# Attention with gradients: the usual path last in the branch, three loads per head in single gated bursts, two transposes of the tail ahead

## The chip, the cores and the metric

The kernel runs on one core of a Trainium2 chip. The metric is device time in microseconds (us), the median of the runs given with each number. Two kernels are compared only by runs of the same job, on the same chip, and kernels of different jobs by their ratios to the kernel before. A ratio is the mean time of one kernel's runs over the mean of the other's runs of the same rounds, so it is not quite the ratio of the medians that are quoted; its 95% interval follows it in brackets.

Engines: PE is the TensorE (matmul), PEld its weight loads, DVE the VectorE, ACT the ScalarE, POOL the GpSimd, SP the SyncE, which here issues all DMA transposes. L683 is line 683 of the kernel.

## The reference

One step of a network and all its gradients:

```python
# S = 2048 rows, D = 576, H = 32 heads of Dh = 128, F = 4608, bfloat16
def A(x, k_cache, v_cache, wq, wo):
    q = (x @ wq) split into heads
    p = softmax(q @ k^T * Dh**-0.5)
    o = p @ v
    return (o joined) @ wo
def forward(...):
    xn = layernorm(x)
    s = A(xn, ...)
    g = silu((sigmoid(xn @ w_gate) * (xn @ w_up)) @ w_down)
    return x + s * g
def reference(..., grad_out):          # forward, then jax.vjp of it:
    return out, dx, dK, dV, dwq, dwo, dw_gate, dw_up, dw_down
```

(The layout is shortened; what the argument needs is that each of 32 heads has a score part, which makes o, and a gradient part, which makes dq, dK and dV.)

## The kernel before

A head is worked in 32 **rows** (row tiles of 128 queries): 16 of scores, 16 of gradients. PE is the bound (busy 99% of the span); a head that nothing disturbs takes 94.63 us, 2.957 us a row. A *slab* is one row's 128 x 2048 of P (later dS). It is transposed by a DMA on the SP queue (PT, later dST), and six rows later (the skew) PE reads the transpose as weights in L683. The loads of the next head, the stores of this one and the transposes are fitted in between. Cuts are marked with `# ...`.

```python
def load_wo(hs):
    nf = (DT - 1) * P if KPAD else D               # 512 of the 576 columns
    rows = slice(hs.h * P, (hs.h + 1) * P)
    if nf:
        nc.gpsimd.dma_start(wo_h[:, :nf], A_wo[rows, :nf])        # L171: 128x512
    if KPAD:
        nc.gpsimd.dma_start(wo_h[:, nf + LO:], A_wo[rows, nf:])   # L173: 128x64
def turn_wot(hs):
    nc.sync.dma_start_transpose(hs.woT[:], wo_h[:])               # L208
# ...
def turn_nat(dst, src):                                           # KT<-Kn, VT<-Vn
    nc.sync.dma_start_transpose(dst..., src...)                   # L615
def transpose_slab(hs, qt, name):                                 # PT, dST
    nc.sync.dma_start_transpose(T[:], hs.slabs[qt][:])            # L630
# ...
# class Partial, end of dV (turned is KT) and of dK (turned is VT):
    nc.gpsimd.dma_start(self.out_T, self.turned)                  # L756: 512 KB to kvT_d
# ... plan(h): what is put into which slot; pl is row 16 of head h-1
put(pl, 0, lambda: heads.__setitem__(h, start_head(h)))
for c in range(4):
    put(pl + q(c), 0, lambda c=c: load_k(hd(), c, 4))             # Kn, 4 x 128 KB
    put(pl + q(skew + 3 + c), 0, lambda c=c: load_v(hd(), c, 4))  # Vn, 4 x 128 KB
put(pl + q(4), 0, lambda: load_wo(hd()))
put(pl + q(5), 0, lambda: load_wq(hd()))
put(pl + q(NTH + 3), 0, lambda: turn_nat(hd().KT, hd().Kn))
put(pl + q(skew + 4), 0, lambda: turn_wot(hd()))
# ...
with tc.If(flag > 0) as branch:
    attention(True)          # the usual path
with branch.Else():
    attention(False)
```

(Kn and Vn are K and V as loaded, KT and VT their transposes.)

Of the kernel before, what the change touches and what calls it, by code (L numbers as in the profile page):

```python
# [66 lines left out]
def kernel(  # L67
# [6 lines left out]
    nc = tc.nc  # L74
# [6 lines left out]
    NT = S // P  # L81
# [85 lines left out]
    def load_wo(hs):  # L167
        nf = (DT - 1) * P if KPAD else D
        rows = slice(hs.h * P, (hs.h + 1) * P)
        if nf:  # L170
            nc.gpsimd.dma_start(wo_h[:, :nf], A_wo[rows, :nf])  # L171
        if KPAD:
            nc.gpsimd.dma_start(wo_h[:, nf + LO:], A_wo[rows, nf:])  # L173
# [5 lines left out]
    def load_k(hs, c=0, n=1):  # L179
        load_kv(hs, hs.Kn, A_k_cache, c, n)  # L180

    def load_v(hs, c=0, n=1):
        load_kv(hs, hs.Vn, A_v_cache, c, n)
# [50 lines left out]
    with tc.tile_pool(name="pa", bufs=1) as pa:  # L234
# [265 lines left out]
        wo_h = pdT.tile([P, DT * P], bf, name="wo_h")  # L500
# [92 lines left out]
    def attention(fast):  # L593
        with ExitStack() as es:
# [169 lines left out]
            def put(slot, cols, fn):  # L764
                units.setdefault(slot, []).append((cols, fn))
# [18 lines left out]
            def q(k):  # L784
                return min(k, NT - 1)

            def plan(h):
                b1, b2 = 2 * NT * h, 2 * NT * h + NT
                hd = lambda: heads[h]
                pl = b2 - 2 * NT if h else None  # L790
                if h:
                    put(pl, 0, lambda: heads.__setitem__(h, start_head(h)))
                    for c in range(4):
                        put(pl + q(c), 0, lambda c=c: load_k(hd(), c, 4))
                        put(pl + q(skew + 3 + c), 0, lambda c=c: load_v(hd(), c, 4))
                    put(pl + q(4), 0, lambda: load_wo(hd()))
                    put(pl + q(5), 0, lambda: load_wq(hd()))
                    put(pl + q(NTH + 3), 0, lambda: turn_nat(hd().KT, hd().Kn))
                    put(pl + q(skew + 4), 0, lambda: turn_wot(hd()))
                    for sc in range(NSC):  # L800
                        put(pl + q(skew + 4 + 2 * sc), DT * CH, lambda sc=sc: prep_qt(hd(), sc))
                for qt in range(NT):
                    put(b1 + qt + skew, NT * P // 2, lambda qt=qt: tail1(hd(), qt, 0))
                    put(b1 + qt + skew, NT * P // 2, lambda qt=qt: tail1(hd(), qt, 1))
                for sc in range(NSC):
                    put(b1 + q(sc), DT * CH, lambda sc=sc: prep_dot(hd(), sc))
                    put(b1 + q(sc + 1), nb * P, lambda sc=sc: prep_don(hd(), sc))
                for qt in range(NT):
                    put(b1 + max(qt + 1, q(2 + qt // nb)), 0, lambda qt=qt: scale_don(hd(), qt))
                put(b1 + q(NTH + 3), 0, lambda: turn_nat(hd().VT, hd().Vn))  # L810
                put(b1 + q(NTH + 2), NT * P, lambda: prep_qn(hd()))
                for qt in range(NT):
                    put(max(b1 + qt + 1, b1 + NT - 4 + qt // 2 if qt < NTH else b1 + NT + qt), 0, lambda qt=qt: scale_qn(hd(), qt))
                put(b2 + 1, 0, lambda: post1(hd()))
                parts = {}

                def first(key, rhs, lo, hi, eng, factor=1.0):
                    parts[key] = part_tile()
                    return Partial(hd(), lo, hi, rhs, parts[key], None, None, eng, factor)
                spread(b1 + NTH, lambda: first("v", hd().dOn, 0, NTH, "v"))  # L820
                spread(b2, lambda: Partial(hd(), NTH, NT, hd().dOn, parts["v"], hd().KT, kvT_d[h, 1], None))
                spread(b2 + NTH, lambda: first("k", hd().Qn, 0, NTH, "s", SCALE))
                spread(b2 + NT, lambda: Partial(hd(), NTH, NT, hd().Qn, parts["k"], VT[:], kvT_d[h, 0], None, SCALE))
                for qt in range(NT):
                    put(b2 + qt + skew, NT * P // 2, lambda qt=qt: tail2(hd(), qt, 0))
                    put(b2 + qt + skew, NT * P // 2, lambda qt=qt: tail2(hd(), qt, 1))
# [37 lines left out]
                slot += 1  # L864

    flag = nc.values_load(flag_i[0:1, 0:1], min_val=0, max_val=1, skip_runtime_bounds_check_because="a comparison gives 0 or 1")
    with tc.If(flag > 0) as branch:
        attention(True)
    with branch.Else():
        attention(False)  # L870
    pdT.release()

    def late(name, bufs=1, **kw):
# [8 lines left out]
    with late("pc") as pc, late("pcf") as pcf, \  # L882
# [165 lines left out]
        def turn_rows(dst, src, a, b, n):  # L1048
            nc.sync.dma_start_transpose(dst[:, a * n:b * n, :], src[:, a:b, :].rearrange("p t f -> p (t f)"))  # L1049
# [111 lines left out]
        with late("c2w") as wp, late("c2b") as blk, late("c2s", 2) as sb, late("c2ps", 4, space=PSUM) as ps:  # L1161
# [10 lines left out]
            dqbT2 = blk.tile([P, max(1, NTE) * HG, P], bf, name="dqbT2")  # L1172
            wqT2 = blk.tile([P, HG, D], bf, name="wqT2")

            def dx_more(st, both=False):
                acc = ps.tile([P, WD], f32, name="acc")
                terms = [(dqbT[:, st * HG + hl, :], wqT[:, hl, :]) for hl in range(HG)]
                if both:
                    terms += [(dqbT2[:, st * HG + hl, :], wqT2[:, hl, :]) for hl in range(HG)]
                dx_row(acc, st, terms)  # L1180
                return acc
# [22 lines left out]
                nc.gpsimd.dma_start(o1[st * P:(st + 1) * P, :], dx[:])  # L1204

            NQ = max(1, NT // 4)
            for hg in range(NHG):
                cols = slice(hg * HC, (hg + 1) * HC)
                onb, dqb = onqs[hg % 2]
                final = hg == NHG - 1  # L1210
                early = hg == NHG - 2
                ends = list(range(NTE)) if early else list(range(NTE, NT)) if final else []
                nc.sync.dma_start_transpose(wqT, A_wq[:, cols])  # L1213
                def turn_dq(a, b):
                    for a_ in range(a, b, NQ):
                        turn_rows(dqbT, dqb, a_, min(a_ + NQ, b), HG)
                turn_dq(NTE if final else 0, NTE if early else NT)
                if early:
                    nc.sync.dma_start_transpose(wqT2[:], A_wq[:, (hg + 1) * HC:(hg + 2) * HC])
                    turn_rows(dqbT2, onqs[(hg + 1) % 2][1], 0, NTE, HG)  # L1220
                dwq = wp.tile([P, DT, HC], bf, name="dwq")
                for st in ends[:2]:
                    load_got(st)
                nsteps, step_n = 2 * HG, 0
                wait_n = min(3 if early else 1, nsteps - 2)
                todo_rows = list(ends)
                held = []

                def ends_rows():
                    if todo_rows and step_n >= wait_n:  # L1230
                        for _ in range(-(-len(todo_rows) // max(1, nsteps - step_n - final))):
                            if todo_rows:
                                st = todo_rows.pop(0)
                                finish(st, dx_more(st, early))
                                if st + 2 <= ends[-1]:
                                    load_got(st + 2)
                for hl in range(HG):
                    h = hg * HG + hl
                    lcols = slice(hl * P, (hl + 1) * P)
                    accumulate(ps.tile([P, WD], f32, name="acc"), dqb, xn_all, lcols, dqTs[h % 2])  # L1240
                    nc.sync.dma_start_transpose(dwq[:, :, lcols], dqTs[h % 2][:])
                    if early and hl == min(1, HG - 1):
                        turn_dq(NTE, NT)
                    if final and hl == HG - 1:
                        store_T(out_4, cols, dwq)
                    step_n += 1
                    ends_rows()
                    dwo = sb.tile([P, D], bf, name="dwo")
                    accumulate(ps.tile([P, WD], f32, name="acc"), onb, ds_all, lcols, dwo)
                    nc.gpsimd.dma_start(out_5[h * P:(h + 1) * P, :], dwo[:])  # L1250
                    step_n += 1
                    if hl < HG - 1:
                        ends_rows()
                if not final:
                    if hg + 2 < NHG:
                        load_on(onb, hg + 2)
                        load_dq(dqb, hg + 2)
                    store_T(out_4, cols, dwq)
                    for st in range(len(ends), NT):
                        acc = dx_more(st)  # L1260
                        nc.vector.tensor_tensor(dxn[:, st, :], acc[:, :D], dxn[:, st, :], op=ALU.add)
                while todo_rows:
                    step_n = nsteps
                    ends_rows()
# [30 lines left out]
```

## Time and profile before

| | before |
|---|---|
| median of 4 runs beside the changed kernel's | 4947.94 us (4942.96 to 4948.41) |
| span of the profiled run | 4943.52 us |
| start to first score tile | 482.91 us |
| heads 0 to 31, to the end of the attention | 3053.05 us |
| of it heads 1 to 30, over 30 x 94.63 us | 8.48 us |
| end of the attention to the end of the kernel | 1407.56 us |

The page's first parts, the stretches, PE's waits and the places of the three targets are in the prediction below. In such tables of waits the three numbers are total us, times, and the longest; in a timeline line the first two are start and length, and the bracket is the idle time just before with what ended it. This is the timeline of the kernel before, head 1 (it starts at 573.48 us), the queues of GpSimd and SP:

```profile
643.13 0.55 POOL L756 DMA_DIRECT2D kvT_d<-KQ  x1 [4.58 <-DVE KQ L754]
648.72 0.77 POOL L677 DMA_DIRECT2D dq_d<-dq_n  x1 [5.04 <-ACT dq_n L724]
651.00 2.83 SPq L615 DMA_TRANSPOSE KQ<-Kn  x1
653.92 18.67 SPq L630 DMA_TRANSPOSE dST<-Pq  x8
```

The dV store is issued at row (643.13 - 573.48) / 2.957 = 23.6, as soon as DVE has made dV. It has landed when the K transpose comes up at 651.00 (row 26.2), between the slab transposes, and nobody waits.

### The profile page before, as it was taken

To read this page: it belongs to the slowest core of one execution; us is meant where nothing else is said; L and a number is where in the kernel's file an instruction comes from. 1 tells how busy PE (TensorE), PEld (TensorE's weight loads), DVE (VectorE), ACT (ScalarE), POOL (GpSimd) and SP (SyncE) were. 2 spreads that over 40 slices of the span, in tenths; PEclk is the share of its full clock that TensorE was granted. 3 is DMA by queue.
4 is the path that set the end of the run, shared out by engine and by line. 5 is a ranking of instruction groups with operands and counts; after the bars stand their busy time and mean duration, and the time that the engine had idled before them with its cause. 6 is when DMAs were issued, how large, how long until landed. Compare 5 with 4: busy or idle time off the path is not lost. (4 is left out here: it accounts for less than half of the span.)

```text
span 4943.5 us, 101621 instructions
## 1 busy us (share of the span) xinstructions
PE 4877.6 (99%) x41029; PEld 2892.8 (59%) x41029; DVE 2802.9 (57%) x6554; ACT 2473.9 (50%) x4228; POOL 843.4 (17%) x1329
## 2 busy tenths in 40 slices
PE   9999999999999999999999999999899999999998
PEld 4445666666666666666666666666455555555554
DVE  4544666666566666666656666666434555554225
ACT  4431766766676676676666667667312111111011
POOL 3322111111111111111111111111221111111111
PEclk9999999999999999999999999999999999999999
DMA  7887999999999999999999999999999999998665
GB/s 260 274 202 173 225 222 225 228 229 230 222 231 224 230 225 237 219 227 220 235 220 231 233 224 229 231 221 231 210 225 235 223 234 218 233 226 204 195 168 151
DMA packets 3048181, 1097.68 MB, mean 222 GB/s; under 512 B 2951890, under 2 KB 2956115, under 8 KB 3047699
## 3 DMA queue, kind: packets, MB, share of 16 engines
q1 hardware_dynamic: 2948930, 771.66, 83.4%
q0 software_dynamic: 98160, 318.85, 20.3%
q8 instruction: 322, 5.28, 0.4%
q14 instruction: 161, 1.31, 0.1%
q10 hardware_dynamic: 608, 0.59, 0.0%
HBM read 175.31 MB, written 177.93 MB: 71 GB/s over the span
## 5 line engine op out<-in xcount | busy, mean ns | idle before, releaser
L654 ACT ACTIVATE Pq<-sp 128x1024 bf16<-128x1024 f32 x1024 | 1048.0, 1024 | 268.7 <-PE sp L636 259.4
L709 DVE SCALAR_TENSOR_TENSOR Pq<-dp,negdelta,Pq 128x1024 bf16<-128x1024 f32 x512 | 655.2, 1280 | 44.5 <-PE dp L706 44.5
L712 ACT ACTIVATE t<-dp,negdelta 128x1024 bf16<-128x1024 f32 x512 | 567.6, 1115 | 214.3 <-PE dp L706 199.8
L636 PE MATMUL sp<-KQ 128*128 128x512 bf16 x2048 | 609.6, 379 | 2.2 <-ACT Pq L654 2.1
L706 PE MATMUL dp<-VT,dOT 128*128 128x512 bf16 x2048 | 609.2, 379 | 2.3
L683 PEld LDWEIGHTS <-dST 128*128 128x128 bf16 x8192 | 506.8, 98 | 155.5 <-DMA dST<-Pq 16.3
L683 PEld LDWEIGHTS <-PT 128*128 128x128 bf16 x8192 | 499.8, 98 | 133.6 <-DMA PT<-Pq 14.1
L683 PE MATMUL acc<-Kn,dST 128*128 128x128 bf16 x8192 | 556.3, 219 | 9.0 <-DMA dST<-Pq 8.8
L683 PE MATMUL acc<-Vn,PT 128*128 128x128 bf16 x8192 | 542.0, 219 | 8.6 <-DMA PT<-Pq 8.3
L713 DVE TENSOR_TENSOR Pq<-t,Pq 128x1024 bf16<-128x1024 bf16 x512 | 354.6, 693 | 319.3 <-ACT t L712 307.0
L744 PE MATMUL acc<-Pq,dOn 128*128 128x512 bf16 x2048 | 531.1, 379 | 0.0
L744 PE MATMUL acc<-Pq,Qn 128*128 128x512 bf16 x2048 | 526.7, 380 | 0.0
L724 ACT ACTIVATE dq_n<-acc,rsc 128x128 bf16<-128x128 f32 x512 | 187.7, 367 | 335.1 <-PE acc L683 313.6
L1154 DVE TENSOR_TENSOR dxn<-acc,dxn 128x576 f32<-128x576 f32 x272 | 206.1, 758 | 248.1 <-PE acc L1054 248.1
L744 PEld LDWEIGHTS <-Qn 128*128 128x128 bf16 x2048 | 200.4, 98 | 240.8 <-issue 1.5
L744 PEld LDWEIGHTS <-dOn 128*128 128x128 bf16 x2048 | 198.9, 98 | 233.8
L1116 ACT ACTIVATE ndh<-dh 128x512 bf16<-128x512 f32 x144 | 86.0, 597 | 452.5 <-DVE du_blk L1114 448.7
L641 DVE TENSOR_REDUCE rs_all<-rsp 128x1 f32<-128x2 f32 x512 | 78.4, 153 | 306.4 <-ACT Pq L654 294.8
L636 PEld LDWEIGHTS <-KQ 128*128 128x128 bf16 x2048 | 179.3, 98 | 124.4 <-issue 4.0
L706 PEld LDWEIGHTS <-dOT 128*128 128x128 bf16 x2048 | 178.7, 98 | 124.6 <-issue 12.4
L677 POOL DMA_DIRECT2D on_d<-o_n x128 | 97.4, 761 | 784.3 <-DVE junk L695 460.3
L677 POOL DMA_DIRECT2D dq_d<-dq_n x128 | 98.2, 768 | 721.4 <-ACT dq_n L724 681.7
(208 smaller groups left out, 6827.6 us busy)
## 6 DMA issues: line engine op xcount, KB each, us to landing
out_dram<-kvn POOLq DMA_DIRECT2D x64, 512.0 KB, 4.8
ah<-a_d POOLq DMA_DIRECT2D x18, 1024.0 KB, 9.3
ah<-h_d POOLq DMA_DIRECT2D x18, 1024.0 KB, 11.7
h_d<-h_row POOLq DMA_DIRECT2D x64, 256.0 KB, 3.5
a_d<-a_row POOLq DMA_DIRECT2D x64, 256.0 KB, 3.9
x_all<-in_A_k_cache_dram SPq DMA_DIRECT2D x64, 256.0 KB, 4.0
on_d<-o_n POOLq DMA_DIRECT2D x128, 128.0 KB, 4.6
kvT_d<-KQ POOLq DMA_DIRECT2D x32, 512.0 KB, 5.7
```

The source lines that it names most:

```text
L636: nc.tensor.matmul(sp[:, c * CH:(c + 1) * CH], lhsT=hs.QT[:, qt * P:(qt + 1) * P], rhs=hs.KT[:, hf * HW_ + c * CH: hf * HW_ + (c + 1) * CH ...
L654: nc.scalar.activation(Pq[:, hsl], sp[:], AF.Exp, scale=SCALE, accum_out=hs.rsp[:, hf:hf + 1])
L677: nc.gpsimd.dma_start(dst_d[q0 * P:(qt + 1) * P, hs.h * P:(hs.h + 1) * P].rearrange("(t p) d -> p t d", p=P), buf[:])
L683: nc.tensor.matmul(hs.acc[:, 0, :], lhsT=T[:, kt, :], rhs=rhs[:, kt, :], start=(kt == 0), stop=(kt == NT - 1))
L706: nc.tensor.matmul(dp[:, c * CH:(c + 1) * CH], lhsT=hs.dOT[:, qt * P:(qt + 1) * P], rhs=hs.VT[:, hf * HW_ + c * CH: hf * HW_ + (c + 1) * C ...
L709: nc.vector.scalar_tensor_tensor(Pq[:, hsl], dp[:], hs.negdelta[:, qt:qt + 1], Pq[:, hsl], op0=ALU.add, op1=ALU.mult)
L712: nc.scalar.activation(t[:], dp[:], AF.Identity, bias=hs.negdelta[:, qt:qt + 1], scale=1.0)
L713: nc.vector.tensor_tensor(Pq[:, hsl], t[:], Pq[:, hsl], op=ALU.mult)
L724: nc.scalar.activation(hs.dq_n[:, qt % G4, :], hs.acc[:, 0, :], AF.Copy, scale=hs.rsc[:, qt:qt + 1])
L744: nc.tensor.matmul(self.acc, lhsT=self.nat[:, qt, :], rhs=self.slabs[qt][:, cs], start=(qt == self.lo), stop=(qt == self.hi - 1))
L1116: nc.scalar.mul(ndh[:], dh[:], -1.0)
L1154: nc.vector.tensor_tensor(dxn[:, st, :], acc[:, :D], dxn[:, st, :], op=ALU.add)
```

## The change

Its intent has three parts. **Loads:** K, wo with wq, and V of the next head each load in one burst, held to a row by a *gate*: a one-element copy on GpSimd from a slab of that row into the destination, so that the load is not issued earlier (K comes at a median row of 18.3, the first piece of wo at 21.8, V at 28.4); they are to stand apart from the dK and dV stores. **Branch:** the usual attention path comes last, so that it falls through into what follows and the jump stands at its entry. **Tail:** the last group's wq transpose and first dq transposes are issued earlier.

```diff
-                    for c in range(4):
-                        put(pl + q(c), 0, lambda c=c: load_k(hd(), c, 4))
-                        put(pl + q(skew + 3 + c), 0, lambda c=c: load_v(hd(), c, 4))
-                    put(pl + q(4), 0, lambda: load_wo(hd()))
-                    put(pl + q(5), 0, lambda: load_wq(hd()))
+                    def gated(slot, dst, fn):
+                        def run():
+                            nc.gpsimd.tensor_copy(dst(), heads[h - 1].slabs[slot % NT][0:1, 0:1])
+                            fn(hd())
+                        put(slot, 0, run)
+                    gated(pl + q(1), lambda: hd().Kn[0:1, 0, 0:1], load_k)
+                    gated(pl + q(5), lambda: wo_h[0:1, 0:1], lambda hs: (load_wo(hs), load_wq(hs)))
+                    gated(pl + q(skew + 6), lambda: hd().Vn[0:1, 0, 0:1], load_v)
 ...
-    with tc.If(flag > 0) as branch:
+    with tc.If(flag < 1) as branch:
+        attention(False)
+    with branch.Else():
         attention(True)
-    with branch.Else():
-        attention(False)
 ...
+            def last_turns():
+                nc.sync.dma_start_transpose(wqT2[:], A_wq[:, (NHG - 1) * HC:])
+                turn_rows(dqbT2, onqs[(NHG - 1) % 2][1], 0, NTE, HG)
 ...
-                if early:
-                    nc.sync.dma_start_transpose(wqT2[:], A_wq[:, (hg + 1) * HC:(hg + 2) * HC])
-                    turn_rows(dqbT2, onqs[(hg + 1) % 2][1], 0, NTE, HG)
 ...
+                if hg == NHG - 3:
+                    last_turns()
```

(Cut: the last group reads `wqT2` in place of a transpose of its own, and a case for two groups.)

More of the change, by code (lines that the diff above doesn't have):

```diff
@@ L1173, with dx_more @@
             wqT2 = blk.tile([P, HG, D], bf, name="wqT2")
-            def dx_more(st, both=False):
+            def last_turns():
+                nc.sync.dma_start_transpose(wqT2[:], A_wq[:, (NHG - 1) * HC:])
+                turn_rows(dqbT2, onqs[(NHG - 1) % 2][1], 0, NTE, HG)
+            def dx_more(st, both=False, w=wqT):
                 acc = ps.tile([P, WD], f32, name="acc")
-                terms = [(dqbT[:, st * HG + hl, :], wqT[:, hl, :]) for hl in range(HG)]
+                terms = [(dqbT[:, st * HG + hl, :], w[:, hl, :]) for hl in range(HG)]
                 if both:
@@ L1206 @@
             NQ = max(1, NT // 4)
+            if NHG == 2:
+                last_turns()
             for hg in range(NHG):
@@ L1212 @@
                 ends = list(range(NTE)) if early else list(range(NTE, NT)) if final else []
-                nc.sync.dma_start_transpose(wqT, A_wq[:, cols])
+                if not (final and NTE):
+                    nc.sync.dma_start_transpose(wqT, A_wq[:, cols])
                 def turn_dq(a, b):
@@ L1233, in ends_rows @@
                                 st = todo_rows.pop(0)
-                                finish(st, dx_more(st, early))
+                                finish(st, dx_more(st, early, wqT2[:] if final and NTE else wqT))
                                 if st + 2 <= ends[-1]:
@@ L1261 @@
                         nc.vector.tensor_tensor(dxn[:, st, :], acc[:, :D], dxn[:, st, :], op=ALU.add)
+                if hg == NHG - 3:
+                    last_turns()
                 while todo_rows:
```

## The prediction

> **What bounds the kernel now.** I read the page first, then the waits of the TensorE (PE) alone, then the stretches around its idle time, then the DMA issues around those.
>
> The page's first and second parts:
>
> ```profile
> span 4943.5 us, 101621 instructions
> PE 4877.6 (99%) x41029; PEld 2892.8 (59%) x41029; DVE 2802.9 (57%) x6554; ACT 2473.9 (50%) x4228; POOL 843.4 (17%) x1329
> PE   9999999999999999999999999999899999999998
> ```
>
> PE is idle for 4943.5 - 4877.6 = 65.9 us in all. The change keeps every matmul, so only this idle time, and the half-speed clock that follows it, can be won. The stretches view (PE, PEld, DVE, ACT, POOL busy, then clock, DMA share, GB/s) confirms it: a head of the attention that nothing disturbs lasts 94.63 us and is all matmul.
>
> ```profile
> 861.20:955.90 94.70, 94.63 (x842) 59.41 (x841) 60.66 (x161) 64.48 (x110) 13.87 (x22) 1.00 1.16 227
> 3535.00:3570.00 35.00, 22.92 (x143) 10.81 (x144) 3.79 (x5) 0.70 (x2) 11.06 (x20) 0.80 0.88 202
> ```
>
> The second line is the 35 us after the attention: 12.1 us idle, and a fifth of the clock withheld. Next, PE's own waits:
>
> ```profile
> PE acc L683 <- DMA dST<-Pq: 8.8, 6, 3.5
> PE acc L683 <- DMA PT<-Pq: 8.3, 9, 1.9
> PE acc L1054 <- DMA dqbT<-dqb: 6.2, 2, 3.8
> PE acc L958 <- issue: 5.4, 2, 4.3
> PE acc L958 <- DMA Vn<-in_A_wo_dram: 3.8, 1, 3.8
> ```
>
> These are the change's three targets: transposes of score slabs that land late (attention), the jump at the end of the attention with its late weight loads (L958), and the transposes of dq in the tail (L1054). Rows of the same view that are not its targets: the start (about 11 us), and the last 11 us after the last matmul.
>
> [...] PE meets the branch at 3532.25 us and its first matmul behind it starts at 3536.07; at the entry, where the usual path falls through, the branch at 481.53 costs PE nothing. [...] The trace has stretches of 3.41 us at half clock just after the gaps at 487, 3515, 3543 and 4846 us, and one of 10.24 us at 3557. [...]
>
> **The change, part by part.**
>
> *Loads.* Counted in row tiles of 2.957 us from a head's start (16 for scores, 16 for gradients), the median head issues wo at row 6.8, the four K pieces at 7.1 to 8.0 and the dK store (512 KB) at 8.8: within 6 us 144 + 512 + 128 (dq) + 512 = 1296 KB. Likewise V at 20.9 to 21.8, then the dV store at 23.5. In head 3 the slab transposes choke there (SP queue; start, length):
>
> ```profile
> 784.64 14.51 SPq L630 DMA_TRANSPOSE PT<-Pq  x3
> ```
>
> 4.8 us each; typical is 2.1. The slack of a transpose (from the end of its issue to the first matmul that reads it) is 13 us on rows 0 to 2 and about 5 on rows 8 to 11; 2.1 us is the least there is, being the time to land, and there PE waits. From the starts of the heads, 23 of 31 periods are 94.63 us (head 0, with less to do, has 90.45); the others exceed it by 3.65 (head 3), 2.89 (head 19), 1.02 (14), 0.46, 0.31, 0.11, 0.05: 8.5 us in all.
>
> The new instruction order on GpSimd has K behind the third o store (row 17.8), wo behind the fourth (21.5), the dV store unmoved at 23.5, V at 28, the dK store alone at 8.8. No 512 KB load stands beside a 512 KB store any more, and K and wo leave the worst place. I take 7.5 of the 8.5 us as gone. Head 0 waits 2.85 us more at 505 and 510 us, after K, wo and wq loads that the old order issues at 483 to 489 us; K is now gated away from there: -1.5. The last head loads no K or V; its paced wo loads, 8 us of waits and one half-clock stretch stay: 0. The gates cost GpSimd 31 x 3 copies of 0.18 us (the existing gate at L942), 17 us, and spare it 31 x 6 issues of 0.54 us, 100 us. It is 17% busy, so neither counts. The woT transpose moves to the sixth gradient row, where the SP queue could wait about 1 us for wo to land; there is slack for it. Sum: -9.
>
> *Branch.* At the end of the attention:
>
> ```profile
> 3536.07 2.61 PE L958 MATMUL acc<-dsT,KQ 128*128 128x512 bf16 x20 [1.07 <-issue]
> 3542.99 2.81 PE L958 MATMUL acc<-dsT,KQ 128*128 128x512 bf16 x14 [4.31 <-issue]
> 3543.62 0.56 POOL L933 DMA_DIRECT2D dsg<-dsg_d  x1 [6.98 <-issue]
> ```
>
> PE loses 1.07 + 4.31 us (a second page came late, while a transpose occupied the DMA engines), GpSimd 6.98 us, and with it everything it loads next: wo for Kn and Vn, issued at 3547.9 and 3548.7, land at 3555.4 and 3560.0, where PE waits 1.77 and 3.77 us more. Falling through, PE and GpSimd go on at 3535 and 3536.7. But PE then meets the o transpose that landed at 3543.8 and later the same wo loads, which will land perhaps 5 us sooner, at about 3555, in the denser traffic of the dK store. So the exit wins about 5.5 us (the 12.1 us idle turn into some 7), not all.
>
> The jump now stands at the entry. PE reaches it at 481.53; by the 3.65 us of the old exit it goes on at 485.2 instead of 483.24. ScalarE branches at 483.46 and would go on near 487; its table load began at 485.07, so the first exponential comes at about 488.9 instead of 486.48, and PE's third score tile waits for that: +2.4. [...] Net of the branch: -2.
>
> *Tail.* The 3.80 us wait at 4846.52 is for the last group's dq transpose, third in a row on the SP queue:
>
> ```profile
> 4833.73 3.80 SPq L1049 DMA_TRANSPOSE dqbT<-ah  x2
> 4837.58 2.33 SPq L1219 DMA_TRANSPOSE wqT<-in_A_wq_dram  x1
> 4840.01 4.33 SPq L1049 DMA_TRANSPOSE dqbT<-dqb  x1
> ```
>
> The change issues the last two ahead of the others. But dqb itself lands at 4831.4, so the queue stands still until then, and the order becomes dqb 4831.4 to 4835.7, wq 3.62 to 4839.4, the first half of ah to 4841.3, landing about 2.2 us later at 4843.5. PE wants it at 4841.58: a wait of 1.9 us stays and 1.9 are won. [...] The final group has no wq transpose in front (2.14 us), so its 2.39 us wait at 4896.8 goes nearly whole: 2.2. Sum: -5.8, taken as -5.5.
>
> *Total:* -9 - 2 - 5.5 = -16.5 us on 4947.6, hence **4931 us** (0.33% less).
>
> **The rivals.**
>
> 1. *The waits only move.* A 512 KB burst of K at row 17.8 meets an o store and V at row 28 meets a dq store; the burst is as large as before, and the SP queue is some 80% filled (32 transposes of 2.4 us, in 94.6). For: gradient rows 4 to 8 have slacks of 4 to 6 us now. Against: the slack at rows 16 to 19 is 8 to 9 us and at row 28 about 10, and the waits of before lie where two large transfers meet. It would leave the loads at -2: 4938 us.
>
> 2. *The jump costs as much at the entry as at the exit*, because the first tile of the attention is a chain through all engines (scores, exponential, transpose)[...]. Then the branch is 0 to +5 instead of -2: 4933 to 4938 us.
>
> 3. *The exit was fetch alone.* If the late wo loads and the 7 us of lost clock (a fifth of 35 us) go with it, the exit wins up to 15 us instead of 5.5, and the total is 4921 us. For: all the waits follow the one stall of GpSimd. Against: the loads took 7.5 and 11.4 us to land once issued, which the branch does not alter.
>
> **Range and chances.** Even every target gone at once (17 us in the attention, 12 and 7 at the exit, 6 and 2 in the tail) would be 44 us, 0.9%; a slow-down by 2% would need 3 us more in each of 32 heads, which the slacks do not suggest. So 2% is out of reach either way, save for an accident of 1% each. Within that, the parts err by about 3 (loads), 4 (branch) and 2 us (tail), and the runs of before spread over 5 us: together about 7 to 8 us, or 10 to 11 for 8 in 10. Range 4920 to 4942; faster 0.01, same 0.98, slower 0.01.
>
> **What would show it.** Loads right: the distances between the heads' first score tiles nearly all 94.6 us, waits for PT and dST before 3420 us falling from 9.2 to about 1 us, and no run of three PT transposes longer than 10 us. Branch right: a gap of 2 to 4 us before the first score tiles near 485 us, no "issue" gap at the first L958 matmuls, GpSimd's first load of dsg within 1 us of the dK store, and wo waits of the same kind left. Tail right: the waits for dqbT at L1054 fall from 6.2 to about 2 us and the half-clock stretch after them goes. Wrong: new waits of PE for dST around gradient rows 2 to 6 (rival 1), gaps of over 6 us at the entry or an unchanged pair of gaps at the exit (rival 2), or an exit without waits for wo (rival 3).

Two terms of its sum: about 1 us at the entry, a guess that no trace gave (with it +2.4 came to +3.5, and the branch to -2), and in the tail 1.7 us for a half-clock stretch spared, since it was not shown that a wait of 1.9 us brings none (1.9 + 1.7 + 2.2 = 5.8, taken as 5.5). The sum, -9 - 2 - 5.5 = -16.5 us, contains both; without them it is -9 - 3.1 - 4.1 = -16.2. In rival 2 a part of its reason is cut, and its second form, in which the exit stays as it was. What is called a page there is a transfer of the instruction queue q8, 16,384 bytes each: the second one behind the jump took 2.02 us (3539.60 to 3541.61; the median of all 322 is 1.03), while the o transpose, issued at 3532.62, landed only at 3543.84.

## More of the kernel before

`wo_h`, a single buffer, is loaded by two transfers. And dV is written into the tile KT (the profile calls it KQ), stored from there by L756 on GpSimd, and then overwritten by the next head's K transpose, L615 on SP, which therefore has to wait until that store has landed (after the change it does so in 29 heads, 98.1 us in all).

## The result, and the profile after

The changed kernel takes **4997.11 us** (median of 4, 4985.46 to 5013.48) against 4947.94 us; the ratio is 1.0104 [1.0071, 1.0137]. That is within 2%, as given with 0.98, but slower by 1% where 0.3% less was predicted, and 55 us above the upper end of the range. Output is correct.

The page's first lines after:

```profile
span 4987.4 us, 100702 instructions
PE 4848.2 (97%) x40273; PEld 2898.8 (58%) x41029; DVE 2803.1 (56%) x6554; ACT 2474.0 (50%) x4228; POOL 760.1 (15%) x1236
```

PE's busy time fell although the work is the same: 756 matmul records (41029 - 40273) are missing in this trace. So PE's busy sum is not used below; weight loads are all there, and heads are timed from the first weight load of their score tiles. By segments of the two profiled runs:

| us | before | after | difference | predicted |
|---|---|---|---|---|
| start to first score tile | 482.91 | 485.52 | +2.6 | +3.5 |
| head 0 | 90.57 | 86.24 | -4.3 | -1.5 |
| heads 1 to 30, over 94.63 each | 8.48 | 68.29 | **+59.8** | **-7.5** |
| head 31 | 115.10 | 115.02 | -0.1 | 0 |
| end of the attention to the first dh matmul | 145.80 | 139.11 | -6.7 | -5.5 |
| the middle of the rest | 1148.03 | 1148.03 | 0 | 0 |
| tail | 113.73 | 106.25 | -7.5 | -5.5 |
| span | 4943.52 | 4987.36 | +43.8 | -16.5 |

In this one pair of profiles, every row but one came out as predicted or better; how far that holds in the other traces is said with the parts below. PE's waits after:

```profile
PE acc L683 <- DMA dST<-Pq: 54.6, 25, 6.0
PE acc L683 <- DMA PT<-Pq: 3.8, 1, 3.8
PE acc L961 <- DMA Vn<-in_A_wo_dram: 3.6, 1, 3.6
PE acc L961 <- DMA Kn<-in_A_wo_dram: 2.9, 1, 2.9
PE sp L636 <- issue: 2.5, 1, 2.5
PE acc L1057 <- DMA dqbT<-ah: 2.0, 1, 2.0
```

The waits for PT fell (8.3 to 3.8 us), but those for dST, the transposed gradient slabs, rose from 8.8 to 54.6 us. Half-clock stretches follow them (at 664.0, 766.4, 1158.9 us and five more): over heads 0 to 30 the clock withheld 20.5 us, against 1.7 before. Waits and clock together make the 68 us (part of the withheld clock falls into the waits themselves).

The stretches view after: first head 1 (PE, PEld, DVE, ACT, POOL busy, clock, DMA share, GB/s), then 35 us at the end of the attention:

```profile
571.80:675.30 103.50, 95.39 (x826) 60.20 (x840) 60.64 (x162) 64.47 (x110) 11.18 (x19) 0.97 1.16 209
3593.00:3628.00 35.00, 27.10 (x206) 13.84 (x208) 6.12 (x9) 2.12 (x6) 12.23 (x22) 0.90 0.86 199
```

Head 1 takes 103.6 us here and moves no more bytes than the quiet head of before (209 GB/s x 103.5 us and 227 GB/s x 94.7 us are 21.6 and 21.5 MB). It is slower with the same traffic; a mean over a head can't tell of jams within it. The same timeline as above, now of the changed kernel's head 1 (it starts at 571.76 us):

```profile
647.30 1.24 SPq L208 DMA_TRANSPOSE woT_h<-wo_h  x1
648.64 4.32 SPq L630 DMA_TRANSPOSE dST<-Pq  x2
651.97 0.56 POOL L173 DMA_DIRECT2D wo_h<-in_A_wo_dram  x1 [15.06 <-DMA woT_h<-wo_h]
652.51 0.55 POOL L756 DMA_DIRECT2D kvT_d<-KQ  x1
656.74 2.09 SPq L615 DMA_TRANSPOSE KQ<-Kn  x1
657.17 0.54 POOL L177 DMA_DIRECT2D Vn<-in_A_v_cache_dram  x1 [0.39 <-PE acc L215]
658.92 17.23 SPq L630 DMA_TRANSPOSE dST<-Pq  x6
667.37 1.89 PE L683 MATMUL acc<-Kn,dST 128*128 128x128 bf16 x16 [5.58 <-DMA dST<-Pq]
```

Read it downwards. GpSimd stands still for 15.06 us in front of the second piece of wo (L173), until the wo transpose has landed. Right behind it in the same queue stands the dV store, ready since about row 23.5: it goes at 652.51, row 27.3 instead of 23.6. On the SP queue the two slab transposes end at 648.64 + 4.32 = 652.96, and then the queue does nothing until 656.74: the K transpose waits for the dV store, which lands at 656.72. All slab transposes behind it are late, the next six take 2.9 us each with the V burst on top (2.3 us in the eight of before); the first of them alone takes 5.86 us and lands at 667.32, and PE waits 5.58 us for it at row 32. With 1.58 us of wait before, and 1.7 us for a half-clock stretch (6.83 us from 664.0, of which 3.46 us lie after PE went on), this gives 8.9 us; head 1's excess is 8.94.

SP's waits at L615 (the K and V transposes), first the kernel before, its largest wait for a store:

```profile
SPq L615 <- DMA kvT_d<-VT: 10.9, 25, 2.2
```

and after:

```profile
SPq L615 <- DMA kvT_d<-KQ: 98.1, 29, 5.5
```

The wait for the dV store is new, in 29 heads, 3.4 us each (head 30 has no second wo piece in front of the store, and issues it at row 23.6). Why the second piece waits is in the view of the tile wo_h: the issues with count, duration and first and last start, and who waited for it. After:

```profile
L171 POOL DMA_DIRECT2D wo_h<-in_A_wo_dram x32: 557/557/573, 333.4 to 3448.9; - x32
L173 POOL DMA_DIRECT2D wo_h<-in_A_wo_dram x32: 543/555/582, 334.0 to 3363.0; - x32
...
  POOL wo_h L173: 282.4, 30
```

Both pieces are issued 32 times, but the last L173 comes at 3363.0 and the last L171 at 3448.9, a head later; likewise head 1's second piece is issued at 486.95 and its first at 541.13. The gate writes one element, `wo_h[0:1, 0:1]`, which only the first piece overwrites. Nothing holds the second piece but the wo transpose that reads the buffer, so the scheduler has put it a head early: right behind that transpose in the data's order, and in front of the dV store in GpSimd's. In heads 1 to 29, GpSimd waits there until row 24.6 to 27.1. Before, GpSimd waited for the same transpose too (383.4 us in 30 heads, in front of L171), but at row 6, with nothing urgent behind it.

The other two parts after. Entry and exit in the timeline:

```profile
485.52 0.60 PE L636 MATMUL sp<-KQ 128*128 128x512 bf16 x2 [2.45 <-issue]
...
3594.18 4.33 PE L961 MATMUL acc<-dsT,KQ 128*128 128x512 bf16 x33
3595.98 0.56 POOL L936 DMA_DIRECT2D dsg<-dsg_d  x1
3608.51 0.90 PE L961 MATMUL acc<-Kn,KQ 128*128 128x512 bf16 x6 [2.90 <-DMA Kn<-in_A_wo_dram]
3613.02 1.60 PE L961 MATMUL acc<-Vn,KQ 128*128 128x512 bf16 x6 [3.62 <-DMA Vn<-in_A_wo_dram]
```

The jump is at the entry now (2.45 us). At the exit there is no "issue" gap (1.07 and 4.31 us before), GpSimd goes on 0.55 us after its dK store, and the two wo waits stay. The tail:

```profile
4889.76 4.87 SPq L1052 DMA_TRANSPOSE dqbT<-ah  x2
4895.10 1.15 PE L1057 MATMUL acc<-wdT,dqbT 128*128 128x512 bf16 x8 [2.04 <-DMA dqbT<-ah]
```

One wait of 2.04 us is left of 3.80 and 2.39 us.

### The profile page after: what moved, and what is told of

It is laid out like the page before. It is cut to its first block, busy times and chain, and to the rows that moved or that the text cites. A ratio compares the mean times of both kernels' runs of the same rounds, so it can differ in the third digit from the quotient of the medians. Undisturbed runs are those within 1.5% of the kernel's fastest.

```text
span 4987.4 us, 100702 instructions
## 1 busy us (share of the span) xinstructions
PE 4848.2 (97%) x40273; PEld 2898.8 (58%) x41029; DVE 2803.1 (56%) x6554; ACT 2474.0 (50%) x4228; POOL 760.1 (15%) x1236
## 4 chain that ended last, share of the span: by engine, by line
PE 92%; DMA 4%; DVE 2%; issue 1%; ACT 1%; SPq 0%; POOL 0%; ACTq 0%; POOLq 0%; DVEq 0%
PE acc L683 18%; PE acc L744 17%; PE acc L1001 13%; PE sp L636 8%; PE acc L1057 8%; PE dp L706 8%; PE acc L215 5%; DMA dST<-Pq 4%; PE u_ps L450 3%; PE dh L1114 3%; PE g_ps L448 3%; PE acc L533 3%; PE acc L961 2%; PE acct L145 1%; DVE Pq L709 1%
## 5 line engine op out<-in xcount | busy, mean ns | idle before, releaser
L683 PE MATMUL acc<-Kn,dST 128*128 128x128 bf16 x8192 | 560.9, 220 | 56.7 <-DMA dST<-Pq 54.6
L706 PE MATMUL dp<-VT,dOT 128*128 128x512 bf16 x1919 | 585.7, 381 | 2.0
L636 PE MATMUL sp<-KQ 128*128 128x512 bf16 x1858 | 568.5, 379 | 3.1 <-issue 2.5
L706 PEld LDWEIGHTS <-dOT 128*128 128x128 bf16 x2048 | 181.4, 98 | 125.3 <-issue 13.7
```

Of the source, the lines that this page charges most:

```text
L636: nc.tensor.matmul(sp[:, c * CH:(c + 1) * CH], lhsT=hs.QT[:, qt * P:(qt + 1) * P], rhs=hs.KT[:, hf * HW_ + c * CH: hf * HW_ + (c + 1) * CH ...
L683: nc.tensor.matmul(hs.acc[:, 0, :], lhsT=T[:, kt, :], rhs=rhs[:, kt, :], start=(kt == 0), stop=(kt == NT - 1))
L706: nc.tensor.matmul(dp[:, c * CH:(c + 1) * CH], lhsT=hs.dOT[:, qt * P:(qt + 1) * P], rhs=hs.VT[:, hf * HW_ + c * CH: hf * HW_ + (c + 1) * C ...
```

## The experiments

**Theory:** the second piece of wo, not gated, holds GpSimd's queue in front of the dV store; through the dV tile this stops SP's queue at the K transpose, and the slab transposes come late. **Rival A:** the V burst of 512 KB at row 28 chokes the transposes (rival 1 of the prediction in its plain form). **Rival B:** the wo load in the gradient rows is itself in the way. **Rival C:** the branch or the tail costs it. Excess below is the sum over heads 1 to 30 of what exceeds 94.63 us, from the one profiled run of each kernel; times have 4 runs each.

| run | median us (range) | ratio to before | excess us |
|---|---|---|---|
| before (profiled run above) | 4947.94 | 1 | 8.5 |
| after | 4997.11 (4985.46 to 5013.48) | 1.0104 [1.0071, 1.0137] | 68.3 |
| e7_wo_alone | 5004.65 (5001.78 to 5011.54) | 1.0117 [1.0096, 1.0139] | 76.5 |
| e1_both_gated | 4950.55 (4934.92 to 4966.73) | 0.9996 [0.9966, 1.0026] | 43.9 (its slowest run) |
| e2_old_loads | 4937.74 (4919.66 to 4944.56) | 0.9973 [0.9943, 1.0003] | 7.2 |
| e6_v_late | 4971.68 (4966.66 to 4978.46) | 1.0054 [1.0034, 1.0074] | 45.1 (its fastest run) |
| e5_tail_only | 4939.22 (4932.29 to 4941.03) | 0.9978 [0.9961, 0.9995] | 9.5 |
| e8_kv_alone | 4952.27 (4947.46 to 4957.45) | 1.0007 [0.9990, 1.0024] | 27.4 |
| e9_both_gated_v_late | 4942.84 (4933.26 to 4948.55) | 0.9992 [0.9975, 1.0009] | 13.7 (its fastest run) |
| e10_both_gated_v_early | 4954.09 (4943.52 to 4959.56) | 1.0015 [0.9998, 1.0031] | 21.1 (its fastest run) |
| e14_repaired_k_as_before | 4934.99 (4927.47 to 4945.05) | 0.9973 [0.9942, 1.0003] | 14.6 |
| e11_k_turn_later | 4945.02 (4932.09 to 4962.97) | 0.9974 [0.9950, 0.9999] | 31.5 (its slowest run) |
| e12_old_loads_k_turn_later | 4941.69 (4934.81 to 4943.50) | 0.9973 [0.9951, 0.9995] | 12.4 |
| e13_repaired_k_turn_later | 4954.55 (4945.24 to 4961.76) | 0.9996 [0.9973, 1.0019] | 34.4 (its slowest run) |

The kernel before had medians of 4943.77, 4948.79, 4953.60 and 4950.16 us in the four jobs (e1, e2, e6, e7; e5, e8, e9, e10; e11 to e13; e14), so a median is to be read with the ratio beside it. Excess can be compared only roughly: the kernel before alone had runs from 4941.49 to 4963.46 us in one job, so that a difference of 20 us between two single profiles can be chance.

**e7_wo_alone: the kernel before, with wo and wq gated as in the change, and nothing else.**

```diff
 (before)
-                    put(pl + q(4), 0, lambda: load_wo(hd()))
-                    put(pl + q(5), 0, lambda: load_wq(hd()))
+                    gated(pl + q(5), lambda: wo_h[0:1, 0:1], lambda hs: (load_wo(hs), load_wq(hs)))
```

> The kernel before with one part of the change alone: wo and wq at the gate of row 21, K and V in four pieces as before, old branch order, old tail. Coupling: GpSimd waits for the wo transpose in front of the dV store, which comes at row 25 or later; excess 20 to 60 us, time 4960 to 5000. Rival (bursts of K and V): nothing is lost, excess near 8 us, time 4940 to 4952.

Measured: 5004.65 us, ratio 1.0117, excess 76.5 us. In heads 1 to 29 the dV store is issued at rows 24.8 to 26.9, the K transpose at 26.4 to 29.5, while V loads at row 21 as before. The line of SP's waits:

```profile
SPq L615 <- DMA kvT_d<-KQ: 117.9, 26, 8.6
```

This one line of the change gives its whole loss. K, V, branch and tail are not needed for it: rivals A (alone) and C fall.

**e1_both_gated: the changed kernel, with a second gate element in the part of wo_h that the second piece overwrites.**

```diff
 (after, in gated's run, for wo alone)
+                            if fn is load_wo_wq and KPAD:
+                                z0 = (DT - 1) * P + LO
+                                nc.gpsimd.tensor_copy(wo_h[0:1, z0:z0 + 1], row[0:1, 0:1])
```

> The changed kernel with a second one-element gate on the 64-column piece of wo, so that GpSimd no longer waits for the wo transpose in front of the dV store. Theory (coupling): the dV store goes from row 25.3 back to 23.6 of a head, the K transpose starts at row 26 or before, the excess of the periods of heads 1 to 30 over 94.63 us falls from 68 us to 10 or less, and the kernel takes 4925 to 4940 us. Rival (the 512 KB bursts themselves slow the slab transposes): the dV store moves, but the excess stays above 45 us and the time above 4975 us.

Measured: 4950.55 us, ratio 0.9996: 1.1% of time for one 0.18 us copy per head. In the timeline of its head 1 (start 570.47 us):

```profile
635.05 0.56 POOL L171 DMA_DIRECT2D wo_h<-in_A_wo_dram  x1 [0.18 <-POOL wo_h L803]
635.60 0.56 POOL L173 DMA_DIRECT2D wo_h<-in_A_wo_dram  x1
640.21 0.55 POOL L756 DMA_DIRECT2D kvT_d<-KQ  x1 [4.05 <-DVE KQ L754]
```

The two pieces go together, and the dV store waits for DVE alone again, at row 23.6 (so in 28 of 30 heads). SP's wait for it at L615 is gone from the list. The first and larger piece of wo is moved in the same rows as in the changed kernel, so rival B falls as the main cause. But the expected 10 us of excess were too few: 43.9 us in the profiled run, which is the slowest of the four, with waits mostly at rows 30 to 32 behind the V burst at row 28.4. A second, smaller loss is left in this run.

**e2_old_loads: the changed kernel with the old five load lines; branch and tail alone.**

```diff
 (after)
-                    gated(...)   # all three, and gated itself
+                    for c in range(4): ...   # K, V, wo, wq as before
```

> The changed kernel with the loads as before: branch order and tail only. Both theories put the whole loss on the loads, so the excess of heads 1 to 30 is that of before (about 8 us), the entry costs 2.6 us, the rest after the attention saves 11.8 us: 4938 us, give or take 5. If instead the new branch order hurts the attention, it stays above 4950 us.

Measured: 4937.74 us, ratio 0.9973, excess 7.2 us, as expected. Branch and tail are sound; rival C is out.

**e6_v_late: the changed kernel with V's gate three rows later (row 31.8 instead of 28.4).**

```diff
-                    gated(pl + q(skew + 6), lambda: hd().Vn[0:1, 0, 0:1], load_v)
+                    gated(pl + q(skew + 9), lambda: hd().Vn[0:1, 0, 0:1], load_v)
```

> The changed kernel with the gate of V moved by three row tiles, from row 28 to row 31; the wo pieces as in the change, so the dV store stays late (about row 25). If the V burst on top of the late K transpose is what makes the delay reach TensorE, the excess falls from 68 us to below 25 and the time to about 4945; if the late dV store and K transpose are enough by themselves, it stays at 50 to 70 us and the time at 4980 to 5000.

Measured: 4971.68 us, ratio 1.0054, excess 45.1 us, between the two expectations. The dV store is as late as in the changed kernel. So the V burst adds to the damage when it falls on a queue that is already behind, about half a per cent of the 1.0%; with the store in time (e1 against e9) moving it makes no difference that the intervals show.

**e9_both_gated_v_late: e1 and e6 together.**

```diff
 (after: the second gate element of e1, and)
-                    gated(pl + q(skew + 6), lambda: hd().Vn[0:1, 0, 0:1], load_v)
+                    gated(pl + q(skew + 9), lambda: hd().Vn[0:1, 0, 0:1], load_v)
```

> Both repairs together: the second wo piece gated too (dV store back at row 23.6, as in e1) and V moved from row 28 to row 31 (as in e6). Each alone left about 44 us of excess over heads 1 to 30 in its profile. If the two act in a chain (late K transpose, then V on top of it), together they leave 15 us or less and the time is 4925 to 4940 us. If the K burst at row 18 is a third cause of its own, some 20 us or more stay and it takes 4940 to 4950.

Measured: 4942.84 us, ratio 0.9992, excess 13.7 us. This is the change repaired as well as I could, and even in its fastest run it does not get below the 8.5 us of excess of before. (Some 2 of the 13.7 us are no waits at all: its undisturbed heads take 94.72 us, not 94.63.)

**e8_kv_alone: the changed kernel with wo and wq as before.**

```diff
-                    gated(pl + q(5), lambda: wo_h[0:1, 0:1], lambda hs: (load_wo(hs), load_wq(hs)))
+                    put(pl + q(4), 0, lambda: load_wo(hd()))
+                    put(pl + q(5), 0, lambda: load_wq(hd()))
```

> The changed kernel with wo and wq as before (ungated, near row 7), K and V in gated bursts at rows 18 and 28. No wo load stands in front of the dV store, so it comes at row 23.6. If the coupling through wo and the V burst are the causes, this does as e1 (excess 15 to 45 us, 4935 to 4965 us). If the wo load at row 22 by itself also slows the transposes there, it does better than e1, below 15 us and near 4935.

Measured: 4952.27 us, ratio 1.0007, excess 27.4 us. The dV store is in time (row 23.6 to 24.4), so the coupling is gone. Against e2, which has the same branch and tail, the re-timed K and V save nothing, and by the two profiles they cost (the intervals overlap); the waits are mostly at rows 21 to 27 and 30 to 32.

**e10_both_gated_v_early: e1 with V in one ungated burst at row 21.3.**

```diff
 (e1)
-                    gated(pl + q(skew + 6), lambda: hd().Vn[0:1, 0, 0:1], load_v)
+                    put(pl + q(skew + 3), 0, lambda: load_v(hd()))
```

> As e1, but V in one burst at row 21, where it was before, not at row 28. If the place of V behind the K transpose is what e1 still suffers from, the waits around rows 30 to 32 go; but V, wo and the dV store then stand within three rows and the slack of gradient rows 4 to 8 falls to that of before (about 4 us) or below: excess 10 to 40 us, 4935 to 4960 us. If the K burst is to blame for the rest, it is no better than e1.

Measured: 4954.09 us, ratio 1.0015, excess 21.1 us in its fastest run. The waits have moved with the burst, to rows 23 to 28 in most of the heads that lose. This is rival 1 of the prediction as it was worded: the waits only move.

**e14_repaired_k_as_before: e9 with K in the four ungated pieces of before (rows 7 to 8).**

```diff
 (e9)
-                    gated(pl + q(1), lambda: hd().Kn[0:1, 0, 0:1], load_k)
+                    for c in range(4):
+                        put(pl + q(c), 0, lambda c=c: load_k(hd(), c, 4))
```

> The repaired kernel (both pieces of wo gated, V at row 31.8) with K loaded as before the change, in four ungated pieces, so that wo and V alone are re-timed. Heads 1 to 30 of the repaired kernel lost 13.7 us over 94.63 us each, those of the kernel before 8.5. If the K burst at row 18 is what still costs (the heads of the repaired kernel with a later K transpose stood still at rows 22 to 24): excess at 8 us or less and no waits at rows 18 to 24, time about 4937 us as with the old loads, 0.998 of before. If what is left is the 512 KB V burst or the wo load in the gradient rows: excess 12 to 16 us, waits in rows 22 to 32 as in the repaired kernel, and 4942 us, 0.999. If the K pieces again stand beside the dK store at rows 7 to 9 and choke transposes there: waits at rows 8 to 11, and no gain.

Measured: 4934.99 us, ratio 0.9973, excess 14.6 us. None of heads 1 to 30 waits at rows 18 to 32 any more; the waits are at rows 10 to 18, behind the K pieces and the dK store (near the third case, which gave rows 8 to 11). That the time is nevertheless that of e2 is no contradiction at this precision: its interval overlaps e9's. In these two single runs, then, the K burst at row 18 goes with waits at rows 22 to 31 of e9 (4.1 us of them), and K at row 7 with waits at rows 10 to 18 (9.3 us), and the excess is about the same. The link is not strict: e9 too waits 4.2 us at rows 14 to 18, in two heads, with no K load there.

**e11_k_turn_later: the changed kernel, with the K transpose held back by a gate until after the 11th gradient slab's, instead of the 8th's.**

```diff
-                    put(pl + q(NTH + 3), 0, lambda: turn_nat(hd().KT, hd().Kn))
+                    put(pl + q(11), 0, lambda: (nc.gpsimd.tensor_copy(hd().KT[0:1, 0:1], heads[h - 1].slabs[11][0:1, 0:1]),
+                                                turn_nat(hd().KT, hd().Kn)))
```

> The changed kernel with one difference: the K transpose of the next head stands behind the eleventh gradient row's transpose in the SP queue, not behind the eighth (a one-element gate on its destination, from slab row 11). The wo piece still delays the dV store to row 25 or later. If the delay reaches TensorE because the SP queue stands still at the K transpose until the dV store has landed, it now lands before its turn comes: the excess of heads 1 to 30 falls from 68 us to 30 or below, the time from 4997 to 4955 or below. If it is the traffic of late dV store and V burst that slows the transposes, whatever their order, the excess stays above 50 us and the time above 4975.

Measured: 4945.02 us, ratio 0.9974. The dV store is as late as ever (rows 24.6 to 28.3 in heads 1 to 29), and yet the ratio falls from 1.0104 to 0.9974: the lateness reaches PE only where the K transpose waits at the head of SP's queue. PE's waits in the profiled run, the slowest of the four:

```profile
PE sp L636 <- DMA KQ<-Kn: 16.6, 10, 3.6
PE acc L683 <- DMA dST<-Pq: 13.7, 9, 3.3
```

The wait for dST fell from 54.6 to 13.7 us, and a new one shows the price: in ten cases K lands too late for the next head's first score tiles.

**e12_old_loads_k_turn_later and e13_repaired_k_turn_later: the same gate in e2 and in e9.**

```diff
 (e2; e9)
-                    put(pl + q(NTH + 3), 0, lambda: turn_nat(hd().KT, hd().Kn))
+                    put(pl + q(11), 0, ...)   # as in e11
```

> Old loads, new branch order and tail (e2: 4938 us), with the K transpose three places later in the SP queue. The slack of gradient rows 8 and 9, 4 us at the median in the kernel before, should rise by some 2 us, the excess of heads 1 to 30 fall from 7 us to 5 or less: 4930 to 4938 us. If the SP queue only shifts its delay to rows 11 and after, it takes 4938 to 4945.

> The change with all repairs: second wo piece gated, V at row 31, K transpose three places later. Without the K transpose in the way the excess of e9 (14 us in its profile) should fall to 5 or less: 4925 to 4938 us, the fastest of all. If the K burst at row 18 is what is left, it stays at 10 to 20 us and the time at 4935 to 4945.

Measured: e12 4941.69 us, ratio 0.9973, the same as e2: where the store is in time, the later K transpose shows no gain. e13 4954.55 us, ratio 0.9996, excess 34.4 us: a miss. Three heads lose 7.0, 7.8 and 10.5 us, with waits at rows 22 to 24 (8.51 us in head 24 alone), that is before the K transpose and its gate, and after the K burst. By time e13 is not worse than e9 (0.9996 and 0.9992, overlapping intervals): the two excesses come from its slowest run and e9's fastest. What differs in the traces is the landing of the K burst. In the three heads (24, 22, 20) it took 15.9, 12.7 and 14.3 us, 6.3 at the median; in e9 never more than 7.4. In head 24, from 2828 to 2840 us, the DMA engines were as busy as ever (share 1.13 to 1.39) but moved 74 to 84 GB/s. In all traces of gated K, the twelve bursts that took over 10 us fell in heads that lost 2.5 to 11.0 us. Why some bursts are so slow, the record does not show.

**e5_tail_only: the kernel before with the tail part of the change** (its edit is the `last_turns` part of the diff above).

```diff
 (before)
+            def last_turns():
+                nc.sync.dma_start_transpose(wqT2[:], A_wq[:, (NHG - 1) * HC:])
+                turn_rows(dqbT2, onqs[(NHG - 1) % 2][1], 0, NTE, HG)
```

> The kernel before with the earlier transposes of the tail alone (old loads, old branch order). The stretch from the first matmul of the next-to-last group to the end was 113.7 us before and 106 us in the changed kernel: this should show 105 to 110 us, the entry and the exit of before, and 4940 us, give or take 4. If the tail saves nothing by itself, 4944 to 4948.

Measured: 4939.22 us, ratio 0.9978 [0.9961, 0.9995]. The tail segment is 106.8 us (113.7 before); entry 482.87 and exit 145.4 us are those of before. It, e11 and e12 are the three versions that are faster than the kernel before by an interval that excludes 1 (e11 barely, at 0.9999); all have the new tail. The branch on top of the tail (e2 against e5) brings nothing that the intervals show.

## Why the prediction was wrong, point by point

**The loads: wrong, and the whole miss.** The step that failed is "The new instruction order on GpSimd has K behind the third o store (row 17.8), wo behind the fourth (21.5), the dV store unmoved at 23.5, V at 28". Three of the four rows were right (K 18.3, wo 21.8, V 28.4). The dV store was not: it went at a median row of 25.3, up to 27.3. The step took "wo" as one transfer. It is two, and the gate covers one; the other, a head early and waiting for SP's wo transpose, stood in front of the dV store in that very order of instructions, and the step passed over it. The same paragraph says that for the wo transpose "the SP queue could wait about 1 us ...; there is slack for it": the question was asked of the wrong queue. SP waited for wo only 2.5 us in all; GpSimd waited for SP's transpose (282 us in 30 heads), and SP then for GpSimd's store (98 us in 29 heads). e7 shows that this is enough for the loss, e1 that it is the missing gate element, e11 that the path to PE is the K transpose in SP's queue. The prediction's sign of a loss, waits for dST at gradient rows 2 to 6, missed the place too: 47 of the 51 us of waits in heads 1 to 30 start between rows 29 and 32 (gradient rows 13 to 16), behind the K transpose.

The dV store, ready at row 23.6, left 0.54 us after the piece in front of it in GpSimd's queue (652.51 - 651.97), once that piece's wait of 15.06 us had ended.

**The gain of 7.5 us from separating loads and stores: wrong too, if smaller.** With the coupling repaired (e9) heads 1 to 30 lose 13.7 us in its fastest run, not 1. For every place of a 512 KB transfer that I tried, the profile shows waits near it: K at row 18 at rows 22 to 28, K at row 7 at rows 10 to 18, V at 21 at rows 23 to 28, V at 28 at rows 30 to 32. That speaks for rival 1, which I had put at 7 us of the time and set aside. It is not shown beyond these single runs: the ratios of e1, e8, e9, e10 and e14 (0.9973 to 1.0015) hardly separate them from each other or from the kernel before.

**Head 0: right in mechanism, mis-sized.** -4.3 us against -1.5: with K and wo gated away, the two waits at 505 and 510 us (2.85 us) went whole. Another 1.5 us is not won by the loads: PE's third score tile waits 0.61 us for ScalarE, 2.12 before, since PE starts 2.6 us later and ScalarE's first exponential only 1.65 us (488.13 for 486.48).

**The entry: right in mechanism, mis-sized.** +2.6 against +3.5 us at the first score tile; PE's gap is 2.45 us. At the third tile, for which +2.4 was worked out (its own numbers, 483.46 + 3.65 against 485.07, give +2.0), only 1.65 us are left (489.28 for 487.63). So entry and head 0 together gave -1.7 us where +2.0 was predicted. Rival 2 (the jump as dear at the entry as at the exit) falls: 2.45 us against 1.07 + 4.31. PE's branch instruction at the entry, taken now, lasts 4.00 us (from 481.46) and was over in 0.09 us before (at 481.53); at the old exit, where it was taken, it lasted 3.65 us (from 3532.25), and PE has none there now.

**The exit: right in mechanism, its size in part luck.** -6.7 against -5.5 us. The wo waits stay as predicted (2.90, 3.62 and, for the o transpose, 1.18 us, together 7.7 where "some 7" were given), and the clock is 0.90 in that stretch, 0.80 before. Rival 3 (all 15 us) falls. The "issue" gap is gone in all 11 traces with this branch order, but from the end of the last attention matmul to the first dh matmul they take 139.6 (the changed kernel, the least) to 146.3 us (e1), against 146.1 to 147.6 us in the three with the old order: the gain is between nothing and 8 us.

**The tail: right in mechanism, a little low.** -7.5 against -5.5 us; 2.04 us of wait are left (1.9 predicted), without a half-clock stretch. That last point held by little: in three others of the 12 traces with this tail (e2, e11, e13), after waits of 2.2 to 3.2 us, the half clock is there.

Without the loads of heads 1 to 30 the parts predicted -9.0 us and gave -16.0 (+43.8 - 59.8). The range failed because its parts were given errors of 2 to 4 us each, while a queue that stops in each of 30 heads multiplies: 2 us a head are 60 us. The prediction had written that a slow-down would need a loss in each head, "which the slacks do not suggest"; slacks hold for transposes that are issued in time, and say nothing of a queue that stands still.

**What stays open:** why some K bursts land so late, and whether the spread of e1 (4935 to 4967 us) and of e11 is such bursts falling in more or fewer heads; e1's slowest run has two of them, and these heads lose 4.2 and 11.0 us.

## What to carry to other kernels

Where a gate holds a load by writing one element of its destination, check that every transfer into that tile overlaps the element: here a tile that is filled by two transfers needed two gates (1.0104 with one, 0.9996 with both), for the free one was issued a head early, behind the tile's last reader. Before moving a transfer, list for each queue what stands behind every wait in it, and follow the ring (here GpSimd to SP to GpSimd to SP) until it ends on an engine with slack. A loss that recurs per head deserves a wider range than one that occurs once.

## What these traces show of queues, branches and the clock

- GpSimd's issue that waited (15.06 us in head 1) held back the issues behind it in its queue. A 16 KB piece (128 x 64 bf16) held a 512 KB store by up to 3.7 rows (row 27.3 for 23.6, 11 us), and cost 1.0% of the kernel, with no more bytes moved in head 1 than in a quiet one (21.6 and 21.5 MB).
- Of the two instruction queues one, q8, moves 16,384 bytes at a time (322 times before), the other, q14, 8,192 bytes (161 times on the page). That q8 is PE's is my estimate, from PE's 82,058 matmuls and weight loads, 255 for each of the 322, and from a q8 transfer that starts at 482.59 us, 1.13 us after the taken branch at the entry, where the kernel before has none between 479.29 and 502.7.
- PE's branch instruction lasted 0.09 us where it fell through (before, entry) and 3.65 us (before, exit) and 4.00 us (after, entry) where it was taken. PE lost 2.45 us at the entry, and 1.07 and then 4.31 us at the old exit, where the second q8 transfer took 2.02 us to arrive (1.10 and 0.98 for those before and after it) while the o transpose was landing (issued at 3532.62, landed at 3543.84).
- The half-clock stretches last 3.413 us or a whole multiple of it (6.83, 10.24), save one that runs into the end of each trace, and lie on one grid: those at 664.0, 1158.9 and 1353.4 us begin 145 and 202 times 3.413 us apart. Gaps of 2.45 us (485.52) and 2.68 us (1352.11) were followed by half clock, where most of one window of that grid was idle, while a gap of 3.32 us (3276.89), split over two windows (idle 46% and 51%), was not. Cutting the traces of before and after, from the attention's start to PE's last matmul, into such windows: PE was idle for 62 to 77% of the 5 full-clock windows of before that half clock followed, and for 59 to 100% of the 12 of after; of the other 1,290 and 1,287 full-clock windows the most idle had 56% and, right at the edge, 59% (4893.1 us).
